# Threshold attention and a causal mixture of attention experts on one core: the mask moved from TensorE to VectorE, the threshold to GpSimd, the first pair in fp32, and a new order

## The chip, the cores and the metric

The kernel runs on one core of one Trainium2 chip. The metric is device time in microseconds (us), as a median of runs; lower is better. The engines are TensorE (PE in the rows; its weight loads are PEld), VectorE (DVE), ScalarE (ACT), GpSimd (POOL) and SyncE (SP), which issues the transfers (SPq is its queue).

## What is computed

Two attentions follow each other, for 8 batches. The first has 8 heads of 64 columns over 576 positions, and keeps only the scores within `tau` of the row's maximum. Its output, with the heads side by side, is the input of four expert attentions with a causal mask, of which each position takes the two that a gate ranks highest:

```python
scores = scale * q @ k.T
thresh = max(scores, -1) - tau
scores = where(scores >= thresh, scores, -1e9)
attn = exp(scores - max(scores)); attn /= sum(attn) + 1e-9
x = attn @ v                                  # heads side by side: 8 x 576 x 512
# experts e = 0..3, gate: two of four by x @ w_gate, softmax over the two
q, k, v = x @ wq[e], x @ wk[e], x @ wv[e]
scores = where(causal, -1e9, scale * q @ k.T)
a = exp(scores - max(scores)); a /= sum(a) + 1e-9
out += weight[e] * (a @ v @ wo[e])
```

All of it is fp32.

## The kernel before

The work of the first attention is cut into 32 pairs of heads (four pairs for each batch). A pair has nine head-tiles of 128 queries by 576 keys: four query tiles for each of two heads, and one tail tile that holds the last 64 queries of both. After four pairs comes the MoE stage of their batch: two pairs of experts, each with five query tiles.

`prep` loads and prepares a pair. To multiply in fp32r (a rounded fp32 that TensorE takes in one pass) without losing digits, each operand is transposed on TensorE and split into a high part (a ScalarE copy) and a low part (a VectorE subtraction), `hl`. Twelve SyncE transfers then spread them over the partitions, into `kt` (8) and `qt` (4). The query is scaled by `qsc` beforehand (`perm`, on GpSimd, for pair 0 on VectorE).

`scores` handles a head-tile: four matmuls (six for the tail tile, on `qd` and `hl`) into two banks of PSUM; a VectorE reduction gives the negated maximum (L525); a one-column VectorE operation gives the threshold `thr` (L517, `tau_p`); ScalarE takes the exp (L551); a VectorE operation with two inputs keeps exp where the score reaches the threshold and sums it (L539); after two heads VectorE inverts the sums (L515, L528) and GpSimd scales the tile (L517). `transp` transposes the result on TensorE and ScalarE copies it to `pt` (L488). `attnv` multiplies with the values.

`moe` runs `projected` and `values` (queries, keys, values, gate), `spread2` (transfers), then `scores2` for each tile: matmuls in fp32r; one bf16 matmul for each head adds the causal mask to the diagonal 128 columns, as `mask` times the identity `ident_b` (for the tail tile 64 columns of `mask2`); one reduction gives both heads' negated maxima; exp with a sum on ScalarE; inversion on VectorE; scaling by the gate on GpSimd. Then transposes, values, and `output`.

The order is not written by hand. Each operation goes into a list (`Plan.op`) with its engine and a guessed duration, from `cost`, `run`, `matmul` and `dma`. `Plan.arrange` then simulates five engines. TensorE takes its groups strictly by a rank, which is the pair's number plus an entry of `PLACE`; the others take the ready operation with the least rank (plus an entry of `PLACE_OP`). The program of each engine is what comes out, and on the chip each engine follows its own list in order. Buffers come from families with the counts in `SLOTS`; "s" is a tile of two banks, "g" of one.

Of the kernel before, what the change touches and what calls it, by code (L numbers as in the profile page):

```python
# [46 lines left out]
    "vload": 0.0126,  # L47
}
PLACE_OP = {
    "ACT gw": 0.9726, "ACT hl": 1.7382, "ACT lg": 0.8296, "ACT p2": -0.4951, "ACT pp": -0.1064, "ACT pt": -0.18,  # L50
    "ACT ptt": 0.0089, "ACT q2": -0.8434, "ACT q2d0": 0.5848, "ACT q2d1": 0.4564, "ACT v2": -0.3794,
    "ACT warm": -0.0714, "ACT wkh": -0.3286, "ACT woh": 0.3985, "ACT wqh": -0.7887, "ACT wvh": 0.8437,
    "ACT x": -0.737, "ACT z0": 0.6018, "ACT z1": 0.3857, "DVE col": 0.4443, "DVE gate": 0.6395, "DVE gt": -1.0307,
    "DVE gw": -0.8879, "DVE hl": -0.7751, "DVE lg": -0.0765, "DVE pp": -0.3478, "DVE pt2t": 0.6626,
    "DVE q2": 1.2382, "DVE qd0": -2.4916, "DVE qi": -1.5694, "DVE qsc": -0.8621, "DVE st": -0.6224,
    "DVE tau_p": 0.8442, "DVE tm": 1.5092, "DVE v2": 0.3515, "DVE warm": -0.6351, "DVE x": -1.4136,
    "DVE z0": 0.1452, "DVE z1": -0.7086, "POOL hl": -1.7102, "POOL ident": -0.1344, "POOL ident_b": 0.2099,
    "POOL ki": -0.3582, "POOL mask": -1.1453, "POOL mask2": -0.772, "POOL p2": 1.2822, "POOL pp": 0.981,
    "POOL q2d0": 0.2142, "POOL q2d1": 1.651, "POOL qd0": 0.9441, "POOL qd1": -0.1544, "POOL qi": 1.7205,
    "POOL st": 0.3311, "POOL tie": -0.8985, "POOL tm": 0.3736, "POOL vtz0": -0.1835, "POOL vtz1": -1.1581,  # L60
    "POOL wkl": 1.6919, "POOL wol": -0.3468, "POOL wql": 2.3927, "POOL wvh": -0.2524, "POOL wvl": 2.8955,
# [3 lines left out]
}  # L65
AV_GROUPS = ((4, 0, 1), (2, 3))
AV2_GROUPS = ((4, 3), (2, 1, 0))

# [319 lines left out]
def kernel(  # L388
# [670 lines left out]
    for n in range(NPR):  # L1059
        pair(n)  # L1060
        if n == 0:
            later()
            for c in range(NC):
                load_weights(c, 1.0 + 0.3 * c)
# [38 lines left out]
```

## Time and profile before

| | |
|---|---|
| median of 3 runs | 950.55 us (950.45 to 952.97) |
| the profiled execution | 949.99 us |
| its span, first to last instruction | 948.3 us |
| busy: TensorE / VectorE | 913.8 / 745.8 us |
| busy: ScalarE / GpSimd | 657.2 / 397.3 us |
| mean granted TensorE clock | 0.996 |

A busy share is an average over stages; what an edit is worth is read from the stage in which its instructions stand. Matmuls are pipelined: the duration of a row is from its start to its modelled end, and the spacing of starts tells what a slot costs. "Idle before" is the time in which the engine stood ahead of an instruction, with what ended it.

### The profile page before, as it was taken

How to read it: one execution, taken by the hardware profiler on the slowest of the kernel's cores; microseconds unless marked ns; L12 is line 12 of the kernel's file. 1: busy time of each engine (PE TensorE's matmuls, PEld its weight loads, DVE VectorE, ACT ScalarE, POOL GpSimd, SP SyncE). 2: the span in 40 equal slices, each digit the busy share in tenths (PEclk: the TensorE clock that was granted, in tenths of full speed). 3: DMA queues.
4: the chain of work that ended last, by engine and by line, in shares of the span. 5: the costliest groups of instructions: out<-in, count | busy, mean ns of one | idle time of the engine just before them, and what ended most of it. 6: DMA issues, size and time to landing. Idle time of an engine off the chain costs nothing.

```text
span 948.3 us, 26245 instructions
## 1 busy us (share of the span) xinstructions
PE 913.8 (96%) x9360; PEld 846.5 (89%) x9360; DVE 745.8 (79%) x2192; ACT 657.2 (69%) x1528; POOL 397.3 (42%) x664
## 2 busy tenths in 40 slices
PE   4798999999999999999999999999999999999998
PEld 3687999899999998999999999989999899999986
DVE  4799878887889868797878877888788886889254
ACT  3677777786678766787667866678566776678443
POOL 3674435453355434354244533445235443334122
PEclk9899999999999999999999999999999999999999
DMA  6766564545555453744636456354464645360151
GB/s 151 199 172 151 128 157 111 128 118 132 140 149 144 129 120 89 185 123 122 141 93 163 110 137 170 100 148 119 118 152 132 152 111 120 89 156 21 35 150 51
DMA packets 125122, 121.27 MB, mean 128 GB/s; under 512 B 67136, under 2 KB 83264, under 8 KB 124992
## 3 DMA queue, kind: packets, MB, share of 16 engines
q1 hardware_dynamic: 124992, 119.60, 50.3%
q8 instruction: 74, 1.21, 0.6%
q14 instruction: 56, 0.46, 0.1%
HBM read 30.42 MB, written 9.44 MB: 42 GB/s over the span
## 4 chain that ended last, share of the span: by engine, by line
PE 79%; DVE 10%; ACT 3%; SPq 3%; DMA 2%; issue 2%; POOL 1%; DVEq 0%; ACTq 0%; POOLq 0%
PE banks L468 60%; PE banks L1072 19%; DVE col L525 4%; DVE pp L539 3%; SPq L561 2%; ACT pt L488 1%; SPq L563 1%; ACT pp L551 1%; DMA st<-in_moe_wq_dram 1%; DMA k2x<-q 1%; DVE x L499 1%; DMA st<-in_moe_wk_dram 1%; DVE col L517 0%; DVE gt L490 0%; DVE col L515 0%
## 5 line engine op out<-in xcount | busy, mean ns | idle before, releaser
L517 POOL TENSOR_SCALAR pp<-pp,col 128x576 f32<-128x576 f32 x288 | 212.6, 749 | 271.2 <-DVE col L528 225.6
L525 DVE TENSOR_REDUCE col<-banks 128x1 f32<-128x576 f32 (+4 forms) x368 | 276.5, 761 | 56.2 <-PE banks L468 54.9
L551 ACT ACTIVATE pp<-banks,col 128x576 f32<-128x576 f32 (+2 forms) x296 | 215.2, 736 | 73.9 <-DVE col L525 60.4
L539 DVE SCALAR_TENSOR_TENSOR pp<-banks,col,pp 128x576 f32<-128x576 f32 x288 | 231.1, 814 | 38.1 <-ACT pp L551 32.9
L488 ACT ACTIVATE pt<-banks 128x512 f32<-128x512 f32 (+2 forms) x400 | 218.7, 588 | 48.7 <-PE banks L1072 46.7
L468 PE MATMUL banks<-kt,qt 128*128 128x288 f32 x1024 | 191.2, 317 | 7.6 <-DVE pp L539 3.8
L1072 PE MATMUL banks<-ident,pp 128*128 128x128 f32 x1326 | 192.0, 276 | 6.1 <-DVE pp L539 2.5
L1072 PEld LDWEIGHTS banks<-ident,pp 128*128 128x128 f32 x1326 | 154.9, 142 | 12.3 <-POOL pp L517 5.1
L468 PEld LDWEIGHTS banks<-kt,qt 128*128 128x128 f32 x1024 | 146.4, 193 | 19.1 <-DVE pp L539 5.5
L468 PE MATMUL banks<-pt,vm 128*64 128x128 f32 (+1 forms) x2560 | 155.1, 265 | 1.1 <-DMA vm<-in_v_dram 1.1
L468 PEld LDWEIGHTS banks<-pt,vm 128*64 128x64 f32 x2560 | 130.9, 137 | 9.7 <-issue 6.1
L517 POOL TENSOR_SCALAR p<-p,col,gw 128x512 f32<-128x512 f32 (+3 forms) x120 | 72.7, 614 | 97.6 <-DVE col L517 42.6
L551 ACT ACTIVATE p<-banks,col 128x512 f32<-128x512 f32 (+4 forms) x136 | 74.7, 555 | 30.3 <-DVE col L525 27.8
L468 PE MATMUL banks<-k2x,q2x 128*128 128x256 f32 (+3 forms) x256 | 62.2, 355 | 4.2 <-DMA k2x<-q 2.4
L468 PE MATMUL banks<-wvh,x 128*128 128x260 f32 x320 | 65.5, 288 | 0.0
L1072 PE MATMUL banks<-ident,p 128*128 128x128 f32 x386 | 60.4, 273 | 0.4 <-POOL p L517 0.3
L468 PE MATMUL banks<-woh,z 128*128 128x512 f32 x160 | 59.1, 413 | 1.5 <-DVE pp L539 1.5
L488 ACT ACTIVATE hl<-banks 128x512 fp32r<-128x512 f32 (+1 forms) x96 | 47.4, 494 | 18.2 <-PE banks L1072 13.3
L499 DVE TENSOR_TENSOR hl<-banks,hl 128x512 fp32r<-128x512 f32 (+1 forms) x96 | 52.8, 550 | 8.1 <-ACT hl L488 5.1
L468 PE MATMUL banks<-ptt,vtz 128*64 128x128 f32 (+1 forms) x640 | 59.0, 262 | 0.0
L517 DVE TENSOR_SCALAR col<-col,tau_p 128x1 f32<-128x1 f32 x288 | 55.4, 206 | 1.8
L468 PE MATMUL banks<-x,wkh 128*128 128x288 f32 x256 | 54.4, 304 | 0.0
(106 smaller groups left out, 1442.3 us busy)
## 6 DMA issues: line engine op xcount, KB each, us to landing
kt<-hl SPq DMA_DIRECT2D x256, 144.0 KB, 2.7
qt<-hl SPq DMA_DIRECT2D x128, 128.0 KB, 2.4
k2x<-q SPq DMA_DIRECT2D x128, 128.0 KB, 2.3
qi<-in_q_dram SPq DMA_DIRECT2D x64, 128.0 KB, 2.6
vm<-in_v_dram SPq DMA_DIRECT2D x32, 256.0 KB, 3.2
q2x<-q SPq DMA_DIRECT2D x64, 128.0 KB, 2.4
out_dram<-st SPq DMA_DIRECT2D x32, 256.0 KB, 2.4
km<-in_k_dram SPq DMA_DIRECT2D x31, 256.0 KB, 3.2
```

What stands on the lines that cost most here:

```text
L468: lambda o, x, y: nc.tensor.matmul(o, x, y, start=start, stop=stop))
L488: run(e, t, [dst], [src], lambda d, s: nc.scalar.activation(d, s, AF.Copy))
L499: lambda d, a, b: (nc.vector if e == "DVE" else nc.gpsimd).tensor_tensor(d, a, b, op=op))
L517: m.tensor_scalar(d, s, x_, y_, op0=op0, op1=op1)
L525: lambda d, s: nc.vector.tensor_reduce(d, s, axis=axis, op=op, **({"negate": True} if negate else {})))
L539: nc.vector.scalar_tensor_tensor(d, a_, x_, r.pop(0), op0=op0, op1=op1, **kw)
L551: nc.scalar.activation(d, s, AF.Exp, **kw)
L561: fn = lambda d, s: q_.dma_start(d.bitcast(F32), s.bitcast(F32))
L563: fn = lambda d: q_.dma_start(d, src)
L1072: o.fn(*(r.place() for r in (*o.outs, *o.ins)))
```

## The change

The causal mask is no longer a matmul. The query weights are negated, so that PSUM holds negated scores. For a tile of `scores2` one VectorE operation for each head adds the mask (now +1e9 above the diagonal, zeros before it, 512 columns wide), writes the sum back into PSUM and takes the minimum, which is the negated maximum that exp needs as its bias; exp then has the factor -1. The tail tile gets a VectorE addition of 64 columns, and a reduction as before. The threshold's one-column operation goes to GpSimd. Pair 0 is prepared by a new `first`: its operands are transposed and copied in fp32, without splitting and without spreading transfers, and each score half is one fp32 matmul; its query loads, and that of tau, are issued by ScalarE. The guessed durations change a little, `PLACE` may hold entries for a single pair (`s00@1`), and both tables of the order have new numbers.

```diff
@@ class Op
+        own = f"{self.unit}@{self.base:g}"
+        self.unit = own if own in PLACE else self.unit
@@ def matmul
-            t, more = 60, 145
+            t, more = 106, 145
+        elif w == HS and x.dtype == F32:
+            t, more = 4 * w * 0.43 + 9.5, 162
@@
+    def masked_min(s, m, least):
+        run("DVE", cost("DVE", size(s), True, True), [s, least], [s, m],
+            lambda o, a, i, m: nc.vector.tensor_tensor_reduce(o, i, m, 1.0, 3e38, ALU.add, ALU.min, a))
@@
-    mask = const("mask", [P, P], BF16)
+    mask = const("mask", [P, SM], BF16)
@@ def load_weights
-        for w, wh, wl, sc in ((wq, wqh, wql, SCALE), (wk, wkh, wkl, 1.0), (wv, wvh, wvl, 1.0)):
+        for w, wh, wl, sc in ((wq, wqh, wql, -SCALE), (wk, wkh, wkl, 1.0), (wv, wvh, wvl, 1.0)):
@@
+    def first():
+        plan.place = (-9.5, "load")
+        tl = plan.tile("tm", [P, 2, D], F32)
+        ki, qi = (plan.tile(f, [P, R, 2, D], F32) for f in ("ki", "qi"))
...
+        for j in range(2):
+            dma(ki[:, :, j], ks[:, :, j])
+            dma(qi[:, :, j], qs[:, :, j], "ACT")
+        dma(tl[ST:], k[0, :2, SM:, :].rearrange("h s d -> s h d"))
+        dma(tl[:ST], q[0, :2, SM:, :].rearrange("h s d -> s h d"), "ACT")
...
+        for x, name in ((ki, "kT"), (qi, "qT")):
...
+            for r in range(R):
+                transpose(g[:, r * P:(r + 1) * P], x[:, r].rearrange("p j d -> p (j d)"))
+            if x is ki:
+                copy("ACT", kx[:, ST:ST + SM], g)
+            else:
+                scaled("DVE", qx[:, :SM], g, qsc, 0.0, ALU.mult, ALU.add)
...
+        return (qx, kx, qd, None, *values_in(0))
@@ def scores
-            k_ = 2 if s < R else 3
+            k_ = 0 if n == 0 else 2 if s < R else 3
+            for hf in range(2 if n == 0 else 0):
+                sl = heads[j] if s < R else slice(0, P)
+                o = hf * HS + (ST if j == 0 else 0)
+                matmul(sp[:, hf, :HS], qt[sl, s * P:(s + 1) * P] if s < R else qd, kt[sl, o:o + HS], True, True)
@@
-            scaled("DVE", thr[:, js], nmx[:, js], -1.0, tau_p, ALU.mult, ALU.subtract)
+            scaled("POOL", thr[:, js], nmx[:, js], -1.0, tau_n, ALU.mult, ALU.add)
@@ def scores2
-                    matmul(g[:, j], q2x[:, j, t * P:w], k2x[:, j, i, :w], i == 0, False)
-                matmul(g[:, j, t * P:w], ident_b, mask, False, True)
+                    matmul(g[:, j], q2x[:, j, t * P:w], k2x[:, j, i, :w], i == 0, i == 1)
             views = [g[:, j] for j in range(2)]
-            reduce(nmx, g, AX.X, ALU.max, negate=True)
+            for j, sv in enumerate(views):
+                masked_min(sv, mask[:, SM - w:], nmx[:, j:j + 1])
...
-            matmul(g[:, 1, HS - ST:HS], ident_b, mask2, False, True)
+            edge = g[:, 1, HS - ST:HS]
+            tt("DVE", edge, edge, mask2, ALU.add)
...
-                reduce(nmx[:, :1], sv, AX.XY, ALU.max, negate=True)
+                reduce(nmx[:, :1], sv, AX.XY, ALU.min)
```

## Rows read from the trace of the kernel before

**Rows 1.** The page's first part: the span, then busy us of each engine.
```profile
span 948.3 us, 26245 instructions
PE 913.8 (96%) x9360; PEld 846.5 (89%) x9360; DVE 745.8 (79%) x2192; ACT 657.2 (69%) x1528; POOL 397.3 (42%) x664
```
**Rows 2.** Busy time by stage: window, length, engines, granted clock, DMA share, GB/s.
```profile
15.00:25.00 10.00, 7.54 (x29) 6.82 (x30) 7.01 (x19) 4.99 (x9) 3.80 (x8) 1.00 0.75 176
25.00:50.00 25.00, 19.93 (x185) 17.95 (x185) 19.44 (x57) 17.00 (x34) 17.98 (x28) 0.86 0.80 204
50.00:100.00 50.00, 45.15 (x495) 40.64 (x496) 46.01 (x140) 37.79 (x80) 29.73 (x53) 1.00 0.60 148
...
300.00:400.00 100.00, 99.54 (x1027) 93.78 (x1026) 80.19 (x241) 71.57 (x168) 41.62 (x67) 1.00 0.53 134
...
910.00:930.00 20.00, 18.09 (x158) 15.71 (x157) 11.50 (x31) 13.44 (x44) 7.84 (x12) 1.00 0.42 106
```
**Rows 3.** Timeline of TensorE: start, length, operation; the tail tiles of three pairs.
```profile
12.20 1.96 PE L468 MATMUL banks<-hl,qd 128*128 128x288 f32 x6 [0.78 <-POOL ki L517]
...
39.66 1.07 PE L468 MATMUL banks<-hl,qd 128*128 128x288 f32 x6
...
97.55 1.06 PE L468 MATMUL banks<-hl,qd 128*128 128x288 f32 x6
```
**Rows 4.** The clock: a one-microsecond stage, and matmuls early and late in the timeline.
```profile
29.00:30.00 1.00, 0.55 (x3) 0.55 (x4) 0.90 (x5) 0.44 (x1) 0.82 (x2) 0.50 0.92 247
...
21.16 3.32 PE L468 MATMUL banks<-kt,qt 128*128 128x288 f32 x12 [0.52 <-DVE hl L499]
...
29.45 4.32 PE L1072 MATMUL banks<-ident,pp 128*128 128x128 f32 x19 [2.46 <-DVE pp L539]
...
240.09 1.30 PE L468 MATMUL banks<-kt,qt 128*128 128x288 f32 x8
```
**Rows 5.** Groups by line and shape: count, busy us, mean ns, idle before and releasers.
```profile
L539 DVE SCALAR_TENSOR_TENSOR pp<-banks,col,pp 128x576 f32<-128x576 f32 x288 | 231.1, 814 | 38.1 <-ACT pp L551 32.9 <-issue 1.5
...
L517 POOL TENSOR_SCALAR pp<-pp,col 128x576 f32<-128x576 f32 x288 | 212.6, 749 | 271.2 <-DVE col L528 225.6 <-PE banks L1072 15.6 <-DVE col L515 15.1
...
L468 PE MATMUL banks<-mask,ident_b 128*128 128x128 bf16 x128 | 29.5, 230 | 0.0
...
L525 DVE TENSOR_REDUCE col<-banks 128x2 f32<-128x1024 f32 x16 | 19.5, 1220 | 3.0 <-PE banks L468 2.8
...
L517 POOL TENSOR_SCALAR wvh<-lg 128x4 fp32r<-128x4 f32 x4 | 0.8, 199 | 0.0
```
**Rows 6.** Timeline of TensorE around a mask matmul in the last MoE.
```profile
907.38 0.40 PE L468 MATMUL banks<-woh,z 128*128 128x512 f32 x1
907.61 0.40 PE L468 MATMUL banks<-wol,z 128*128 128x512 f32 x1
...
909.25 0.71 PE L468 MATMUL banks<-k2x,q2x 128*128 128x512 f32 x2
909.80 0.23 PE L468 MATMUL banks<-mask,ident_b 128*128 128x128 bf16 x1
909.84 0.48 PE L468 MATMUL banks<-k2x,q2x 128*128 128x256 f32 x2
```
**Rows 7.** Timeline of VectorE: a threshold and the reduction behind it.
```profile
24.55 0.21 DVE L517 TENSOR_SCALAR col<-col,tau_p 128x1 f32<-128x1 f32 x1
24.68 0.74 DVE L525 TENSOR_REDUCE col<-banks 128x1 f32<-128x576 f32 x1
```
**Rows 8.** Timeline: a GpSimd scale and a VectorE multiplication at the same time.
```profile
29.57 1.47 POOL L517 TENSOR_SCALAR pp<-pp,col 128x576 f32<-128x576 f32 x2 [0.18 <-DVE col L528]
29.69 0.82 DVE L539 SCALAR_TENSOR_TENSOR pp<-banks,col,pp 128x576 f32<-128x576 f32 x1
```
**Rows 9.** Timeline: the issue of the first query loads and their first use.
```profile
2.69 1.15 SPq L563 DMA_DIRECT2D qi<-in_q_dram  x2
...
6.06 0.49 DVE L517 TENSOR_SCALAR qi<-qi,qsc 128x512 f32<-128x512 f32 x1 [0.16 <-DMA qi<-in_q_dram]
```

More of the change, by code (lines that the diff above doesn't have):

```diff
@@ L55 @@
[L55 to L59, printed above, removed]
@@ L506, in scaled @@
         kx, ky = isinstance(x, Ref), isinstance(y, Ref)
-        t = cost(e, size(src), inps(src)) + (20 * kx + 80 * ky if e == "POOL" else 0)
+        t = cost(e, size(src), inps(src)) + (20 * kx + 80 * ky if e == "POOL" else 50 * ky)
         def fn(d, s, *r):
@@ L550, in fn @@
                 kw["bias"] = r.pop(0)
-            nc.scalar.activation(d, s, AF.Exp, **kw)
+            nc.scalar.activation(d, s, AF.Exp, scale=scale, **kw)
         run("ACT", cost("ACT", n, inps(src), accum is not None) + 80, [dst] + ([accum] if accum is not None else []),
@@ L558, in dma @@
         a, b = isinstance(dst, Ref), isinstance(src, Ref)
-        late = 2530 if a and b else 2950 if a else 2250
+        late = 2650 if a and b else 2950 if a else 2250
         if a and b:
@@ L581 @@
     run("POOL", 600, [ident], [], lambda x: make_identity(nc, x))
-    dma(tau_t, bass.AP(tensor=tau.tensor, offset=tau.offset, ap=[[0, P], [1, 1]]))
-    scaled("DVE", tau_p, tau_t, 0.0, op0=ALU.max)
+    plan.place = (-9.45, "load")
+    dma(tau_t, bass.AP(tensor=tau.tensor, offset=tau.offset, ap=[[0, P], [1, 1]]), "ACT")
+    plan.place = (-9.0, "load")
+    scaled("DVE", tau_n, tau_t, -1.0, 0.0, op0=ALU.mult, op1=ALU.min)
     scaled("DVE", qsc, tau_t, 0.0, SCALE, op0=ALU.is_ge, op1=ALU.mult)
@@ L608, in later @@
     def later():
-        plan.place = (0.2, "load")
-        rounded(ident_b, ident)
+        plan.place = (0.0, "later")
         memset("POOL", mask, 0.0)
-        run("POOL", 300, [mask], [mask], lambda o, i: nc.gpsimd.affine_select(
-            out=o, in_=i, compare_op=ALU.is_ge, fill=NEG, base=0, pattern=[[-1, P]], channel_multiplier=1))
+        run("POOL", 300, [mask[:, SM - P:]], [mask[:, SM - P:]], lambda o, i: nc.gpsimd.affine_select(
+            out=o, in_=i, compare_op=ALU.is_ge, fill=-NEG, base=0, pattern=[[-1, P]], channel_multiplier=1))
         memset("POOL", mask2, 0.0)
@@ L623, in later, with load_weights @@
             memset("POOL", t.bitcast(F32), 0.0)
[L625 to L626 removed]
+    def load_weights(c):
+        plan.place = (0.0, f"w{c}")
         sl = slice(c * P, (c + 1) * P)
[L628 removed]
+        for w, wh, wl, sc in ((wq, wqh, wql, -SCALE), (wk, wkh, wkl, 1.0), (wv, wvh, wvl, 1.0)):
             t = plan.tile("st", [P, E, D], F32)
@@ L644, in load_weights, with values_in @@
             minus("POOL", wol[:, c], t, woh[:, c].bitcast(F32))
+    def first():
+        plan.place = (-9.5, "load")
+        tl = plan.tile("tm", [P, 2, D], F32)
+        ki, qi = (plan.tile(f, [P, R, 2, D], F32) for f in ("ki", "qi"))
+        ks = k[0, :2, :SM, :].rearrange("h (p r) d -> p r h d", r=R)
+        qs = q[0, :2, :SM, :].rearrange("h (r p) d -> p r h d", r=R)
+        for j in range(2):
[3 more added lines that the diff above has]
+        dma(tl[:ST], q[0, :2, SM:, :].rearrange("h s d -> s h d"), "ACT")
+        plan.place = (0, "load")
+        kx = plan.tile("p2", [P, 2 * SM], F32)
+        qx = plan.tile("p2", [P, 2 * SM], F32)
+        qd = qx[:, SM:SM + P]
+        plan.place = (0, "perm")
+        memset("POOL", qd, 0.0)
+        for x, name in ((ki, "kT"), (qi, "qT")):
+            plan.place = (0, name)
+            g = gbank()
+            for r in range(R):
[4 more added lines that the diff above has]
+                scaled("DVE", qx[:, :SM], g, qsc, 0.0, ALU.mult, ALU.add)
+        plan.place = (0, "tT")
+        g = gbank()
+        transpose(g[:, :P], tl.rearrange("p j d -> p (j d)"))
+        for j, sl in enumerate(heads):
+            scaled("DVE", qd[sl, j * ST:(j + 1) * ST], g[sl, :ST], qsc[sl], 0.0, ALU.mult, ALU.add)
+        for o in (0, ST + SM):
+            copy("ACT", kx[:, o:o + ST], g[:, ST:P])
+        return (qx, kx, qd, None, *values_in(0))
+    def values_in(n):
+        b, hp = divmod(n, NPAIR)
+        plan.place = (n, "vload")
+        vm = plan.tile("vm", [P, 2, R, D], F32)
+        dma(vm, v[b, 2 * hp:2 * hp + 2, :SM, :].rearrange("h (p r) d -> p h r d", r=R))
+        for j, rows in enumerate((slice(0, ST), slice(ST, P))):
+            dma(vtz[n % 2][rows, j], v[b, 2 * hp + j, SM:, :])
+        return vm, vtz[n % 2]
     def prep(n):
         b, hp = divmod(n, NPAIR)
+        if n == 0:
+            return first()
         hs = slice(2 * hp, 2 * hp + 2)
@@ L654, in prep @@
             to = None
-            if sc is qsc or n == 0:
+            if sc is qsc:
                 to = plan.tile(name + "i", [P, R, 2, D], F32)
-                order_ = "h (r p) d -> p r h d" if sc is qsc else "h (p r) d -> p r h d"
-                src = x[b, hs, :SM, :].rearrange(order_, r=R)
+                src = x[b, hs, :SM, :].rearrange("h (r p) d -> p r h d", r=R)
                 for j in range(2):
                     dma(to[:, :, j], src[:, :, j])
-                if sc is qsc:
-                    plan.place = (n, "perm")
-                    fl = to.rearrange("p r j d -> p (r j d)")
-                    scaled("DVE" if n == 0 else "POOL", fl, fl, sc, 0.0, ALU.mult, ALU.add)
-                    plan.place = (n, "load")
+                plan.place = (n, "perm")
+                fl = to.rearrange("p r j d -> p (r j d)")
+                rounded(fl, fl, sc)
+                plan.place = (n, "load")
             else:
@@ L677, in prep @@
         plan.place = (n, "perm")
-        e = "DVE" if n == 0 else "POOL"
         ql = tl[:ST].rearrange("p j d -> p (j d)")
-        scaled(e, ql, ql, qsc[:ST], 0.0, ALU.mult, ALU.add)
+        scaled("POOL", ql, ql, qsc[:ST], 0.0, ALU.mult, ALU.add)
         hl = plan.tile("hl", [P, 2, 2 * SM + 3 * ST], F32R)
@@ L711, in prep @@
         split(slice(SM, SM + 2 * ST), g[:, :P])
-        e = "DVE" if n == 0 else "POOL"
-        copy(e, hl[:, :, KO + S:], hl[:, :, KO:KO + ST].bitcast(F32))
+        copy("POOL", hl[:, :, KO + S:], hl[:, :, KO:KO + ST].bitcast(F32))
         for j, sl in enumerate(heads):
-            copy(e, qd[sl, :, j * ST:(j + 1) * ST], hl[sl, :, SM:KO].bitcast(F32))
+            copy("POOL", qd[sl, :, j * ST:(j + 1) * ST], hl[sl, :, SM:KO].bitcast(F32))
         spread_keys(0)
@@ L721, in prep @@
         spread_queries(1)
-        plan.place = (n, "vload")
-        vm = plan.tile("vm", [P, 2, R, D], F32)
-        dma(vm, v[b, 2 * hp:2 * hp + 2, :SM, :].rearrange("h (p r) d -> p h r d", r=R))
-        for j, rows in enumerate((slice(0, ST), slice(ST, P))):
-            dma(vtz[n % 2][rows, j], v[b, 2 * hp + j, SM:, :])
-        return qt, kt, qd, hl[:, :, KO + ST:], vm, vtz[n % 2]
+        return (qt, kt, qd, hl[:, :, KO + ST:], *values_in(n))
     def inverse(x):
```

41 lines of the change are left out of this document (23 added, 18 removed), and 57 rows, old and new, of tables (PLACE, PLACE_OP).

## The prediction

> **What bounds the kernel now.** I read the page first: TensorE is busy for 913.8 of 948.3 us, VectorE for 745.8, ScalarE for 657.2, GpSimd for 397.3 [rows 1]. So the question is where TensorE is not fed, and the busy time by stage answers it. From 300 to 400 us, and so in all the middle, TensorE is busy 99.5% and VectorE about 80%: there every matmul slot taken away is time. From 25 to 100 us VectorE is busy about as long as TensorE (46.0 of 50 us from 50 to 100), with TensorE short of work [rows 2]. In the first 25 us nothing is full. From 910 to 930 us TensorE is at 90%, and chains through the other engines count.
>
> Then the landmarks. Each pair begins on TensorE with its tail tile (six matmuls banks<-hl,qd): the first at 12.20, the second at 39.66, the fifth at 97.55 us [rows 3]. So pair 0 takes 27.5 us, pairs 1 to 3 take (97.55 - 39.66) / 3 = 19.3 us each. Beside an MoE stage TensorE alone sets the pace; in these first 97 us something else does.
>
> Last, the clock. One stretch is shown at 0.50, half of full speed (1.2 in place of 2.4 GHz), after TensorE had stood still for some 2.5 us; the stage from 15 to 25 us is shown at 1.00. But twelve 288-column matmuls at 21.16 us took 3.32 us, 0.28 us each, where eight took 1.30 us, 0.16 us each, at 240 us [rows 4]. By durations the clock was low for most of the head, whatever the column says. I go by durations. The Trainium skill (TensorE: Matmul & The Clock Gate, Part 1) has the low clock as the state before activity; the durations agree, the granted column does not; by the column the sum below would be some 3 us lower.
>
> **The change part by part.** *Mask matmuls (128 of 128 columns, 16 of 64) go from TensorE.* The 230 ns of one in the groups [rows 5] is latency, not cost. Cost is the spacing: two 512-column matmuls start 0.23 us apart, so the pair that starts at 909.25 has given its slots by 909.71; the mask starts at 909.80 and the next matmul at 909.84 [rows 6]. That is 0.09 + 0.04 = 0.13 us with the switch to bf16 and back; I take 0.125. Ends: 0.04 (the start-to-start alone, 5.8 us in all) and 0.23 (the whole latency, 33 us). 126 of them lie in the seven batches beside another pair: 126 x 0.125 = 15.8 us. 18 lie in the last MoE, where TensorE partly waits [rows 2]; I count half, 1.1 us. Together 16.9 us.
>
> *What VectorE takes on.* 64 tiles had one reduction over two heads (1.22 us at 2 x 512 columns); now two masked minima write the scores back. The operation is not in the trace. Below it lies the reduction for the same columns (no change), above it two of the 814 ns passes with two inputs and a sum (2 x 576 columns, 1.63 us) [rows 5]. It has two inputs, so I take the upper side, +0.3 us: 64 x 0.3 = 19 us. 16 additions of 64 columns: some 0.2 us each, 3 us. Both stand beside TensorE work in seven batches, where VectorE has about 20% to spare [rows 2]: nothing on the path. In the last MoE the first head's minimum ends earlier than the joint reduction did, the second's later: nothing either way. Cover gone, it would cost 22 us.
>
> *The threshold (288 one-column operations) goes from VectorE to GpSimd.* On VectorE it lasts 0.21 us but the next reduction starts 0.13 us after it [rows 7], so 288 x 0.13 = 37 us are freed. VectorE's net is -15, about 731 us. On GpSimd the nearest row is four columns in 199 ns [rows 5]: 288 x 0.2 = 58 us, and GpSimd comes to 455 us, half of the span. It adds a wait: the masked multiplication (L539) now waits for ScalarE's exp and for GpSimd. Exp takes about as long as one 749 ns GpSimd scale, so a threshold that finds GpSimd inside a scale ends up to 0.2 us late; behind the waiting multiplication on VectorE stand the next tile's reduction, and behind that TensorE, which wants the bank. In the middle the spare of VectorE hides it. In pairs 1 to 3, where VectorE is the pace, nine thresholds less per pair are 9 x 0.13 = 1.2 us, three pairs 3.6 us. Ends: 0 (it comes back as waits) and 3 x (19.3 - 16) = 10, TensorE's own pace for a pair being about 16 us (38 matmuls of 288 columns at 0.133, 50 transposes at 0.11, the values' some 5.5; an estimate from the spacing at full clock).
>
> A row speaks on sharing: a multiplication that ran at 29.69 us beside a GpSimd scale lasted 0.82 us [rows 8], the mean over all being 814 ns with GpSimd busy 42%. The Trainium skill (Perfetto Trace Analysis, Optimizing Scalar/DVE Operations) warns that VectorE and GpSimd share an SBUF port, so that moving work between them may not help. By it the 3.6 us would be nothing and the sum 3.6 us higher; these rows show no such loss for these operations.
>
> *First pair in fp32.* Before, each operand is split in two on ScalarE and VectorE, copied by twelve SyncE transfers, and the keys are loaded after the queries: the query loads were issued at 2.69 to 3.84 and used at 6.06 us [rows 9], the first scores start at 12.20, and pair 0 gives way at 39.66. After, SyncE issues three key loads, ScalarE three query loads beside them; a load used 2.2 us after its issue has ended should be there at about 5 us. (ScalarE issues no load in the trace; taken as SyncE's, the ends below hold the rest.) Transposes, about 1 us at the low clock, and one evacuation, 0.7, for each operand: scores from about 7.8 us, an estimate. A tile is now two fp32 matmuls in place of four; each lies between one and four times the 0.133 us of before, and the diff itself charges four, so I take 1.0 us a tile, 2.0 at the low clock. Three tiles at 2.0 until the clock is up, then VectorE's pace, some 1.5 us (0.75 + 0.81 + 0.09, overlapping): 7.8 + 6.0 + 6 x 1.5 = 22.8, and 2.3 for the last tile's reduction, exp and multiplication: 25. Then pair 1's own splitting on VectorE (1.7) and TensorE's backlog of transposes: pair 1's tail tile at about 29 in place of 39.66, so 10.7 us. Ends: 2 (low clock throughout, backlog at half speed) and 14 (full clock from the start). That SyncE is free of pair 0's twelve transfers costs nothing and lets pair 1's loads go first.
>
> *Signs, mask width, weights' place.* Negated query weights and exp with a factor -1 are the same instructions. The wider mask is written once by GpSimd, under 1 us, long before use: nothing. The new weight positions load on SyncE and GpSimd in the same head; hidden as before.
>
> *The new order.* It cannot be priced from the trace. Where TensorE is 99.5% busy it can hardly win; it could lose or win some 4 us over seven batches (about 0.5 each). I take nothing.
>
> Sum on the profiled execution (949.99 us, 1.7 us more than its span, 0.06% under the median of 950.55): 949.99 - 16.9 - 10.7 - 3.6 = 918.8; I say 919.
>
> **The rivals.** (1) *The head is not shortened*: fp32 scores at the low clock hold TensorE, pair 1 still waits for its transfers, and only 2 us come. 949.99 - 16.9 - 2 = 931. For it: the low clock in the head. Against: VectorE was idle for 5.6 of the 25 us from 25 to 50 [rows 2], so an earlier start is worth something. 14%. (2) *The threshold brings no relief*, VectorE waiting for GpSimd what it saves: 922.4. For it: GpSimd's scales are as long as the exp. 10%. (3) *The head comes to TensorE's pace*: 14 + about 8 us in place of 10.7 + 3.6, so 911 or less. For it: with VectorE lighter, TensorE has the most work of all. 15%. (4) *Slower*: the threshold stands in GpSimd's strict order behind a scale that itself waits, so each of the 288 multiplications starts d late. VectorE then has 731 + 288 d; with the about 25 us at both ends in which it cannot work, it passes 950 from d = 0.67 us. A whole scale, 0.75, gives 731 + 216 + 25 = 972. For it: a GpSimd scale of 749 ns is longer than d, and nothing overtakes it. Against: GpSimd is idle for half the span, and the order can put the threshold ahead of a scale that waits. 5%, of which 1% ends near no change.
>
> **How the numbers follow.** Forecast 56%: 919, its own range 912 to 926. For 8 in 10, I take in rivals 1 to 3 and the unknown order: 907 to 932; the mask's ends (5.8 to 33 us) lie partly beyond. A measurement of this kernel can tell about 0.3%. Faster: 95%. Within 0.3%: 1%. Slower: 4%.
>
> **What would show it.** Mask: the batch period on TensorE falls by 18 x 0.125 = 2.3 us. Head: pair 1's tail tile near 29, the fifth near 83 us, pairs 1 to 3 at about 18.1 us. Threshold: VectorE near 731 us, GpSimd near 455, and no GpSimd among the releasers of L539's multiplication; if it is there with many us, rival 2 or 4 holds. Masked minimum: two of 512 columns under 1.7 us together. The prediction is wrong if the middle's TensorE idle grows beyond 1%, or if the low clock comes back after the head.

## The result, and the profile after

The changed kernel takes 943.88 us (median of 5 runs, 942.60 to 947.33); the kernel before took 952.84 us beside it (950.45 to 954.02). The ratio is 0.9911, 95% interval 0.9892 to 0.9930: 0.9% faster. The prediction said 919, with 907 to 932 as its range: right in sign, and wrong by 25 us.

The profiled execution took 944.42 us. The page's first part, which answers [rows 1]:

```profile
span 942.7 us, 26180 instructions
PE 906.0 (96%) x9214; PEld 840.6 (89%) x9214; DVE 731.0 (78%) x2107; ACT 651.9 (69%) x1528; POOL 471.2 (50%) x952
```

TensorE lost 7.8 us of busy time and the span 5.6 us. VectorE fell to 731.0 us, as forecast; GpSimd rose to 471 (forecast 455). So the work moved as planned, but the time did not follow. That VectorE's sum came out to the microsecond is partly luck: the thresholds are worth 29.2 us of its time (e3 below, 760.2 with them), not 37, and the mask's move 17.5 (e1, 763.3 against 745.8), not 22. Busy time by stage (window, length, PE, PEld, DVE, ACT, POOL, granted clock, DMA share, GB/s), against [rows 2]:

```profile
25.00:50.00 25.00, 20.21 (x189) 16.55 (x190) 18.32 (x47) 16.16 (x34) 19.10 (x38) 0.91 0.69 166
50.00:100.00 50.00, 44.97 (x460) 40.75 (x461) 38.56 (x98) 34.98 (x71) 29.86 (x64) 0.90 0.53 128
...
200.00:300.00 100.00, 98.31 (x1008) 92.39 (x1007) 80.24 (x232) 70.22 (x167) 48.47 (x97) 1.00 0.51 126
300.00:400.00 100.00, 99.83 (x1026) 94.32 (x1025) 81.62 (x240) 72.20 (x172) 50.01 (x102) 1.00 0.54 134
```

The middle is about as full as before. From 25 to 100 us TensorE has no more busy time than before (65.2 us against 65.1), at a lower granted clock in the longer stretch: 0.90 from 50 to 100 us, where it was 1.00. The landmarks of [rows 3] show the same (TensorE's timeline: start, length, operation). The first line is pair 0's first scores, the next two the tail tiles of pairs 1 and 4, the last two those of the first pair of the third and of the eighth batch (pairs 8 and 28):

```profile
9.13 1.32 PE L484 MATMUL banks<-p,p 64*128 64x288 f32 x2 [1.07 <-ACT p L504]
...
31.79 0.40 PE L484 MATMUL banks<-hl,qd 128*128 128x288 f32 x1
...
101.78 0.29 PE L484 MATMUL banks<-hl,qd 128*128 128x288 f32 x1
...
206.91 0.29 PE L484 MATMUL banks<-hl,qd 128*128 128x288 f32 x1
...
765.92 0.29 PE L484 MATMUL banks<-hl,qd 128*128 128x288 f32 x1
```

The last two stand at these times in the kernel before:

```profile
203.44 0.40 PE L468 MATMUL banks<-hl,qd 128*128 128x288 f32 x1
...
768.65 0.40 PE L468 MATMUL banks<-hl,qd 128*128 128x288 f32 x1
```

Pair 1 begins 7.9 us earlier than before, and pair 4 begins 4.2 us later. The five batch periods in between last (765.92 - 206.91) / 5 = 111.80 us in place of 113.04, so a batch is 1.24 us shorter, where 2.3 was forecast. From the last of these lines to the end of the span it is 176.8 us in place of 179.6. The head is most of the 25 us: it gave 4 us away where 14 were to be won. The batches gave half of their forecast in this profile.

In the head TensorE stands still three times for a tile that is not yet scaled (timeline of TensorE; in brackets the idle time before and its releaser). L1134 are the transposes, L533 the scaling on GpSimd; for the first of them the matmul's row names VectorE's L531, which ended at the same time, and the row of its weight load names the scaling:

```profile
24.98 1.54 PE L1134 MATMUL banks<-ident,pp 128*128 128x128 f32 x6 [3.60 <-DVE col L531]
27.18 2.07 PE L484 MATMUL banks<-p,p 64*128 64x288 f32 x8
49.81 4.77 PE L1134 MATMUL banks<-ident,pp 128*128 128x128 f32 x19 [2.75 <-POOL pp L533]
70.32 1.12 PE L1134 MATMUL banks<-ident,pp 128*128 128x128 f32 x4 [3.05 <-POOL pp L533]
```

After each, the granted clock is at the lower level (1.2 GHz): the windows read 0.50.

```profile
25.00:28.00 3.00, 2.76 (x11) 2.00 (x13) 0.15 (x1) 1.26 (x4) 1.51 (x3) 0.50 0.69 153
50.00:54.00 4.00, 3.97 (x18) 3.27 (x18) 0.63 (x4) 2.15 (x6) 2.32 (x4) 0.50 0.76 182
70.00:73.00 3.00, 2.68 (x12) 2.69 (x13) 1.72 (x6) 0.90 (x2) 2.63 (x5) 0.50 0.93 224
```

What GpSimd did before the first of these waits, and who waited for it:

```profile
21.25 0.74 POOL L515 TENSOR_TENSOR wvl<-st,wvh 128x256 fp32r<-128x256 f32 x1 [0.90 <-ACT wvh L504]
21.96 1.26 POOL L515 TENSOR_TENSOR wol<-st,woh 128x512 fp32r<-128x512 f32 x1
23.21 0.27 POOL L533 TENSOR_SCALAR col<-col,tau_n 128x1 f32<-128x1 f32 x1
23.55 0.82 DVE L555 SCALAR_TENSOR_TENSOR pp<-banks,col,pp 128x576 f32<-128x576 f32 x1 [0.81 <-POOL col L533]
```

Two weight splits hold GpSimd for 2 us; the threshold stands behind them, and the masking multiplication behind the threshold. Before the second and the third wait GpSimd does other work: the second scaling follows 0.21 us of idleness, the third follows copies for a coming pair (`hl`, `qd`) and a threshold:

```profile
49.01 1.47 POOL L533 TENSOR_SCALAR pp<-pp,col 128x576 f32<-128x576 f32 x2 [0.21 <-DVE col L544]
...
68.50 0.67 POOL L508 TENSOR_SCALAR qd<-hl 64x128 fp32r<-64x128 f32 x2
```

So there were three suspects: the threshold in GpSimd's queue, the weight splits, and the order that puts these transposes where it does. For the batches there were two: that a mask matmul costs TensorE less than I took, and that the masked minimum on VectorE makes TensorE wait.

### The profile page after: what moved, and what is told of

It is laid out like the page before. It is cut to its first block, busy times and chain, and to the rows that moved or that the text cites. A ratio compares the mean times of both kernels' runs of the same rounds, so it can differ in the third digit from the quotient of the medians.

```text
span 942.7 us, 26180 instructions
## 1 busy us (share of the span) xinstructions
PE 906.0 (96%) x9214; PEld 840.6 (89%) x9214; DVE 731.0 (78%) x2107; ACT 651.9 (69%) x1528; POOL 471.2 (50%) x952
## 4 chain that ended last, share of the span: by engine, by line
PE 77%; DVE 8%; DMA 4%; ACT 4%; issue 3%; POOL 3%; SPq 1%; ACTq 0%; DVEq 0%; POOLq 0%
PE banks L484 57%; PE banks L1134 20%; DVE pp L555 2%; DMA kt<-hl 2%; DVE col L541 2%; DMA qi<-in_q_dram 2%; ACT pp L571 1%; SPq L581 1%; POOL pp L533 1%; ACT pt L504 1%; ACT p L571 1%; DVE col L531 0%; DVE x L515 0%; DVE hl L515 0%; POOL col L533 0%
## 5 line engine op out<-in xcount | busy, mean ns | idle before, releaser
L533 POOL TENSOR_SCALAR pp<-pp,col 128x576 f32<-128x576 f32 x288 | 212.6, 748 | 164.3 <-DVE col L544 113.9
L541 DVE TENSOR_REDUCE col<-banks 128x1 f32<-128x576 f32 x304 | 225.7, 753 | 49.4 <-PE banks L484 45.7
L571 ACT ACTIVATE pp<-banks,col 128x576 f32<-128x576 f32 (+1 forms) x295 | 215.0, 744 | 61.2 <-DVE col L541 52.3
L1134 PE MATMUL banks<-ident,pp 128*128 128x128 f32 x1331 | 197.1, 280 | 16.3 <-POOL pp L533 10.0
L484 PE MATMUL banks<-kt,qt 128*128 128x288 f32 x992 | 184.8, 313 | 5.4 <-DMA kt<-hl 4.5
L1134 PEld LDWEIGHTS banks<-ident,pp 128*128 128x128 f32 x1331 | 154.9, 143 | 33.7 <-POOL pp L533 18.4
L533 POOL TENSOR_SCALAR col<-col,tau_n 128x1 f32<-128x1 f32 x288 | 76.8, 267 | 160.3 <-DVE col L541 149.8
L571 ACT ACTIVATE p<-banks,col 128x576 f32<-128x576 f32 (+4 forms) x137 | 74.7, 551 | 14.6 <-DVE col L531 6.4
L533 POOL TENSOR_SCALAR p<-p,col,gw 128x384 f32<-128x384 f32 (+3 forms) x122 | 73.7, 612 | 18.3 <-ACT pp L571 5.7
L504 ACT ACTIVATE x<-banks 128x256 fp32r<-128x256 f32 (+1 forms) x96 | 28.3, 329 | 70.6 <-PE banks L484 70.6
L515 DVE TENSOR_TENSOR q<-banks,q 128x288 fp32r<-128x288 f32 x64 | 29.0, 452 | 44.7 <-ACT q L504 44.2
L560 DVE CUSTOM_DVE_ANT_0 banks<-banks,mask 128x512 f32<-128x512 f32 (+3 forms) x128 | 61.9, 499 | 1.6
L1134 PE MATMUL banks<-ident,p 128*128 128x128 f32 x381 | 61.1, 276 | 0.9 <-POOL p L533 0.9
```

The costliest lines, as they stand in the source:

```text
L484: lambda o, x, y: nc.tensor.matmul(o, x, y, start=start, stop=stop))
L504: run(e, t, [dst], [src], lambda d, s: nc.scalar.activation(d, s, AF.Copy))
L515: lambda d, a, b: (nc.vector if e == "DVE" else nc.gpsimd).tensor_tensor(d, a, b, op=op))
L533: m.tensor_scalar(d, s, x_, y_, op0=op0, op1=op1)
L541: lambda d, s: nc.vector.tensor_reduce(d, s, axis=axis, op=op, **({"negate": True} if negate else {})))
L560: lambda o, a, i, m: nc.vector.tensor_tensor_reduce(o, i, m, 1.0, 3e38, ALU.add, ALU.min, a))
```

## The experiments

All of them compare with the kernel before on the same chip. The code of the edits is shortened. Unless told otherwise, the order of all instructions on every engine is that of the kernel it is made from, so that one thing changes. Times are medians; a difference between two experiments is taken from their ratios to the kernel before, times 950 us; behind ± stands what the two intervals together leave open.

| kernel | us | before beside it | ratio, 95% interval |
|---|---|---|---|
| changed kernel | 943.88 | 952.84 | 0.9911 (0.9892 to 0.9930) |
| e1_mask_alone | 948.80 | 951.36 | 0.9977 (0.9962 to 0.9991) |
| e2_mask_and_threshold | 969.77 | 951.36 | 1.0192 (1.0171 to 1.0212) |
| e3_threshold_back | 943.67 | 951.36 | 0.9914 (0.9895 to 0.9934) |
| e4_filled_waits | 939.27 | 951.36 | 0.9867 (0.9853 to 0.9881) |
| e5_no_mask | 943.68 | 950.48 | 0.9926 (0.9900 to 0.9953) |
| e6_mask_twice | 955.66 | 950.48 | 1.0061 (1.0036 to 1.0085) |
| e7_splits_twice | 950.28 | 950.48 | 1.0001 (0.9990 to 1.0012) |
| e8_head_reordered | 940.24 | 952.07 | 0.9877 (0.9858 to 0.9897) |
| e9_reordered_and_filled | 940.64 | 952.07 | 0.9886 (0.9866 to 0.9906) |
| e10_split_old_places | 954.72 | 949.97 | 1.0051 (1.0035 to 1.0067) |
| e11_fp32_old_places | 948.63 | 949.97 | 0.9981 (0.9968 to 0.9995) |

**e1: the mask alone, in the old order.**

```diff
-                matmul(g[:, j, t * P:w], ident_b, mask, False, True)
+                # not issued
-            reduce(nmx, g, AX.X, ALU.max, negate=True)
+            # per head: tensor_tensor_reduce(sv, sv, mask, 1.0, 3e38, ALU.add, ALU.min, nmx)
```

> The kernel before, in its own order on every engine; only the causal mask is moved: the mask matmuls of the mixture layers are not issued, the weights of the second queries are negated, and VectorE does two masked minimums where it did one maximum (an addition and a minimum in the tail tile). Theory 1 (the mask's price in the sum was right, the loss is in the head): 16.9 us less than before, some 934 (932 to 937). Theory 2 (the masked minimum lengthens the chain from the second scores to their transposes, so the TensorE time saved is waited away): 942 to 949, and TensorE's waits for the GpSimd scaling of the second probabilities grow. Theory 3 (the new order is what lost the gain): as theory 1, and this kernel is faster than the changed one by 5 us or more.

948.8 us, 2.2 us less than before: theory 1 fell here, and theory 3 with it. The time is that of theory 2, but its wait is not there: TensorE waits 0.7 us for the scaling of the second probabilities, where it was 0.3. TensorE's busy time fell to 906.2 us as in the changed kernel, but the span did not. Where a step was lost, in the MoE stage of the second batch:

```profile
288.09 0.59 PE L468 MATMUL banks<-k2x,q2x 128*128 128x384 f32 x2
289.52 0.41 PE L468 MATMUL banks<-k2x,q2x 128*128 128x384 f32 x1 [0.84 <-ACT pt L488]
290.25 0.41 PE L468 MATMUL banks<-k2x,q2x 128*128 128x384 f32 x1 [0.31 <-DMA k2x<-q]
```

The matmuls that followed at once before now wait for a bank and for a transfer. The order was made for the old timing: TensorE arrives earlier and waits there. Its time without work grew from 34.5 us (948.3 - 913.8) to 43.1 (949.3 - 906.2).

**e5 and e6: the mask's price on TensorE.** In e5 the masks are not issued and nothing replaces them; in e6 each is issued twice.

```diff
             if x.dtype == BF16:
+                nc.tensor.matmul(o, x, y, start=start, stop=False)
```

> The kernel before in its own order, without the mask matmuls and with nothing in their place: the second layer's scores stay unmasked, so the causal mask is left out of what is computed. This gives the price of the 144 mask matmuls on TensorE by itself. By the prediction (0.125 us each in 126 cases): 16.9 us less than before, some 934 to 936. By the steps of 0.06 to 0.07 us per mask that the kernel with the mask alone shows against the kernel before: 8 to 10 us less, 941 to 944. What lies between this time and that of the kernel with the mask alone (948.8) is what the masked minimum costs in that order: 5 to 8 us.

> The kernel before in its own order, with each of the 144 mask matmuls issued twice (masked scores are lower by the constant twice, nothing else differs). By the prediction's price of 0.125 us: 17 to 18 us above before, some 969. By 0.06 to 0.07 us each: 8 to 10 us above, some 960.

Without masks the kernel is 7.0 us faster (4.5 to 9.5), with twice as many 5.8 us slower (3.4 to 8.1). Both medians lie below the lower of the two expectations (8 to 10). In the time of the whole kernel 144 masks are worth 6 to 7 us, 0.04 to 0.05 us each, and not 16.9.

On TensorE itself a mask takes more than that. In the last MoE eight matmuls run without idle time between `woh,z` and `x,wkh`, first with four masks among them (the kernel before, further lines in [rows 6]), then with none (e5):

```profile
908.75 0.61 PE L468 MATMUL banks<-k2x,q2x 128*128 128x512 f32 x2
...
910.56 0.51 PE L468 MATMUL banks<-x,wkh 128*128 128x288 f32 x2
```

```profile
904.88 1.54 PE L468 MATMUL banks<-k2x,q2x 128*128 128x512 f32 x8
906.26 0.43 PE L468 MATMUL banks<-x,wkh 128*128 128x288 f32 x2
```

1.81 us against 1.38: 0.43 for four masks, 0.11 each. Part of it comes behind the mask: two matmuls directly behind one take longer than two that follow a matmul of their own kind (0.71 us at 909.25 against 0.61 at 908.75, 0.51 against 0.43 for `x,wkh`). The two programs issue the same matmuls in the same order but for the masks; over the 135 masks with no idle time beside them in either trace, the starts give 0.09 us each, some 13 us for 144. A second mask takes less, as no such switch is added (e6):

```profile
278.86 0.23 PE L469 MATMUL banks<-mask,ident_b 128*128 128x128 bf16 x1
278.93 0.22 PE L470 MATMUL banks<-mask,ident_b 128*128 128x128 bf16 x1
```

It starts 0.07 us behind the first here, 0.06 in other places. The Trainium skill (TensorE: Matmul & The Clock Gate, "Wait — 56ns, not 53.3ns?") gives some 56 ns from start to start for 128 columns at the full clock; these starts lie a little above it. So e6 prices a mask beside a mask, and e5 the mask.

Why e5 gains 7 us and not 13: TensorE has 11.3 us less busy time than before, and its time without work grew by 6.6 us, from 34.5 to 41.1 (943.6 - 902.5); its waits for the keys' transfer into `k2x` alone grew from 2.4 to 5.3 us:

```profile
PE 902.5 (96%) x9216; PEld 840.7 (89%) x9216; DVE 746.2 (79%) x2192; ACT 656.6 (70%) x1528; POOL 397.3 (42%) x664
```

The masked minimum in the old order costs e1 less e5, 0.51% or 4.8 us (± 2.9; expected 5 to 8). So in e1 what the mask's removal brings and what its replacement costs nearly cancel.

**e2 and e3: the threshold.** e2 adds the threshold on GpSimd to e1, at the place where VectorE had it; e3 does the reverse in the changed kernel.

```diff
-            scaled("POOL", thr[:, js], nmx[:, js], -1.0, tau_n, ALU.mult, ALU.add)
+            nc.vector.tensor_scalar(thr, nmx, -1.0, tau_n, op0=ALU.mult, op1=ALU.add)   # e3, same place
```

> As the kernel with the mask alone, still in the order of the kernel before, and the threshold goes from VectorE to GpSimd at the same place of the order. Theory 1: 0 to 4 us less than with the mask alone (the term of 3.6 us for pairs 1 to 3, or nothing where TensorE is the bound). Rival (the threshold in GpSimd's queue is what cost the gain): 3 us or more above the mask alone, with TensorE waiting for the scaled tile behind it.

> The changed kernel in its own order, but the threshold is computed on VectorE again. Theory 1 (GpSimd's weight splits and the order make the three waits of the head): the waits at 21, 47 and 67 us stay; VectorE has 288 small instructions more; 944 to 948. Rival (the threshold in GpSimd's queue costs the gain): 930 to 941, the new wait of the masking multiplication for GpSimd (13.6 us in all) gone and with it most of the three waits of TensorE.

e2 is 20 us slower than e1, far beyond what I expected of the rival. Its waits of VectorE, and its middle (engine, tile and line of the waiting group, releaser: us in all, times, longest):

```profile
DVE pp L539 <- POOL col L772: 31.8, 48, 2.7
300.00:400.00 100.00, 97.66 (x983) 91.00 (x980) 77.70 (x230) 69.61 (x165) 49.04 (x99) 1.00 0.48 119
```

In an order not made for the move, GpSimd meets the threshold late: that is the cause that rival 4 of the prediction named. That its figure (972) lies close to the 969.77 us measured here is luck. It had VectorE full and each of the 288 multiplications starting 0.75 us late; here 48 of them wait, 31.8 us in all or 0.11 us a multiplication, and VectorE is busy 77.7 of 100 us in the middle. In the changed kernel, whose order was made for it, the same group waits 13.6 us:

```profile
DVE pp L555 <- POOL col L533: 13.6, 13, 1.7
```

And there the move is worth nothing. With the threshold back on VectorE (760.2 us busy) the time is 943.67 us against 943.88 (by the ratios 0.3 us more, ± 2.6; theory 1 had said 944 to 948), and the three waits stay as they were (TensorE's waits from 12 to 110 us):

```profile
PE banks L1135 <- POOL pp L533: 9.8, 8, 3.1
PE banks L1135 <- DVE col L531: 4.0, 1, 4.0
```

So the threshold is not what spoils the head in this order; the first suspect is out.

**e7: the weight splits.** Each low half of the weights is computed twice on GpSimd.

```diff
-            minus("POOL", wl[:, c, :E * D], tf, wh[:, c, :E * D].bitcast(F32))
+            twice(wl[:, c, :E * D], tf, wh[:, c, :E * D].bitcast(F32))   # same tensor_tensor, issued two times
```

> The changed kernel in its own order, but GpSimd makes each low half of the weights in the head twice over (16 subtractions of 0.74 to 1.26 us more, 13 to 14 us of GpSimd time). If GpSimd's weight work in front of the scaling is what makes TensorE's three waits of the head: these waits grow together by 3 us or more and the time by 3 to 8 us, 947 to 952. If the waits come from the place that the order gives to the three transposes, and GpSimd has room: within 1 us of the changed kernel, 943 to 945.

950.28 us, 0.9% or 8.6 us (± 2.1) above the changed kernel. GpSimd has 14 subtractions and 10.9 us more (482.1 us against 471.2), less than the 16 and 13 to 14 expected. TensorE's waits for a scaled tile from 12 to 110 us grow from 12.7 to 20.0 us, first the changed kernel (with the first wait under L531's name), then e7:

```profile
PE banks L1134 <- POOL pp L533: 9.1, 7, 3.0
PE banks L1134 <- DVE col L531: 3.6, 1, 3.6
```

```profile
PE banks L1140 <- POOL pp L533: 20.0, 9, 4.7
```

So GpSimd has no room in the head: 10.9 us more of its work cost 8.6. That the splits as they stand make the three waits does not follow, and the rows above speak against it. For the first wait the inverted sums were there at 22.74 us and the scaling began at 23.46, so a split and the threshold held it for 0.7 of the 3.60 us; no split stands right ahead of the other two scalings.

**e4: the clock after the waits.** Transposes of the identity are put ahead of the three transposes that wait.

```diff
+    fill = {118: 30, 424: 24, 673: 26}    # first transposes of pair 0, 1 and 2 that wait
...
             o = plan.ops[n]
+            for _ in range(fill.get(n, 0)):
+                x = ident.place()
+                nc.tensor.transpose(o.outs[0].place(), x, x)
```

> The changed kernel, but ahead of the three transposes of the head for which TensorE stood idle (21.4, 47 and 67 us) it transposes the identity 30, 24 and 26 times into the same bank, which the real transposes then overwrite; all else as in the changed kernel. If the low clock after each wait is a loss of its own: the stretch after each runs at full rate, 4 to 8 us less, 936 to 940. If the engines ahead of TensorE set the pace of the head anyhow, so that the low clock costs nothing: 943 to 945, and the time goes into longer waits.

939.27 us, 0.44% or 4.2 us (± 2.2) less than the changed kernel, though TensorE does 80 transposes more. The stretches of 0.50 are at 1.00 (the last line is the timeline behind the first of them); in the head a lower reading is left ahead of them, 0.66 from 20 to 25 us:

```profile
25.00:28.00 3.00, 2.61 (x23) 2.21 (x22) 0.59 (x2) 0.98 (x2) 2.09 (x4) 1.00 0.65 146
50.00:54.00 4.00, 2.94 (x25) 2.61 (x24) 0.68 (x1) 2.75 (x8) 2.25 (x4) 1.00 0.61 138
70.00:73.00 3.00, 2.55 (x22) 2.31 (x21) 2.38 (x5) 2.58 (x6) 2.70 (x7) 1.00 0.87 211
27.50 1.25 PE L484 MATMUL banks<-p,p 64*128 64x288 f32 x8
```

The same eight fp32 matmuls take 1.25 us here, and 2.07 us above. So each of these waits cost itself and then the low clock behind it, which is a loss of its own. The planner in this file charges a wait as a wait, with the same matmul costs after it.

**e8 and e9: another order of the head.** e8 changes only the constants in `PLACE` for pairs 0 to 3, for the loads and for the weights; e9 adds one filling of 24 transposes.

```diff
+PLACE.update({"s20@0": ..., "t01@1": ..., "load@2": ..., "w0": ..., ...})   # pairs 0 to 3 and weights only
```

> The changed kernel with the same instructions; only the places in the order of the first four pairs, of the weights and of the loads in the head are others. They were chosen so that, with TensorE at half rate after each long wait counted in, the planner leaves one wait of TensorE above 2 us in the head (before the transposes of pair 0's second tile) in place of three. If the order of the head is what lost the gain: the fifth tail tile at 90 to 94 us in place of 101.78, the low clock after 47 and 67 us gone, 932 to 937. If the head is bound by the work of the engines and the order only moves the waits: 941 to 945.

> As the reordered head, and 24 transposes of the identity ahead of the one transposition for which TensorE still waits over 2 us. If the low clock after a long wait is a loss of its own: 1 to 2.5 us less than with the reordered head alone. If what follows that wait is bound by other engines: the same time within 0.5 us.

e8 takes 940.24 us, 3.2 us (± 2.6) less than the changed kernel, between the two expectations. Its profile has one wait above 2 us behind the start in place of three (3.87 us); its fifth tail tile starts at 98.99 us in place of 101.78, not at 90 to 94. So the order holds part of the loss, and the expectation was too high. e9 gained nothing over e8 (ratios 0.9886 and 0.9877): in its profile the fifth tail tile comes at 97.60 us, 1.4 us earlier, and the gain goes between pairs 6 and 7, where TensorE waits for the spread keys and then runs some 3.4 us at the lower clock, as it does not in e8's profile (1.00 from 170 to 185 us):

```profile
175.68 0.50 PE L515 MATMUL banks<-kt,qt 128*128 128x288 f32 x2 [1.59 <-DMA kt<-hl]
177.00:181.00 4.00, 4.00 (x56) 4.00 (x56) 3.21 (x9) 0.74 (x1) 1.18 (x3) 0.57 0.37 115
```

**e10 and e11: the first pair, and what the new order is worth.** Both have the changed kernel's mask and threshold, and the planner works with the places of the kernel before; e10 prepares the first pair as before, e11 in fp32.

```diff
+PLACE.update({...}); PLACE_OP.update({...})    # e10, e11: the values of the kernel before
-        if n == 0:                             # e10 only: prep() of the kernel before
-            return first()
```

> The changed kernel with the first pair prepared as before (operands split in two, four matmuls a tile) and with the table of places of the kernel before, from which the planner makes an order that keeps pair after pair in sequence. The mask and the threshold are as in the changed kernel. It is the partner of the next run, which has the first pair in fp32 and the same table. In the head: fifth tail tile near 97 us, as in the kernel before (97.55). Time 945 to 955, since this table was not made for these instructions.

> The same table of places, with the first pair straight in fp32. If the fp32 first pair is worth what the prediction said, once the head keeps its sequence: pair 0 ends and every later pair begins 8 to 11 us earlier than in the partner, and the time is as much lower. If the head is not shortened whatever the order (rival 1): 0 to 3 us. What the changed kernel's new table gave away in the head is then the difference of its fifth tail tile (101.78) to this run's: 10 us or more by the first, less than 5 by the second.

The tail tiles of pairs 1 and 4, first e10, then e11; the last two lines of e11 are the third and eighth batch (pairs 8 and 28):

```profile
42.04 1.14 PE L486 MATMUL banks<-hl,qd 128*128 128x288 f32 x6
102.31 1.06 PE L486 MATMUL banks<-hl,qd 128*128 128x288 f32 x6
```

```profile
34.81 1.07 PE L486 MATMUL banks<-hl,qd 128*128 128x288 f32 x6
95.76 1.06 PE L486 MATMUL banks<-hl,qd 128*128 128x288 f32 x6
201.85 0.40 PE L486 MATMUL banks<-hl,qd 128*128 128x288 f32 x1
765.83 1.06 PE L486 MATMUL banks<-hl,qd 128*128 128x288 f32 x6
```

e10 missed one of its expectations: its fifth tail tile stands at 102.31 us, not near 97. With the first pair in fp32, pair 1 begins 7.2 us earlier and pair 4 6.6, and 0.70%, 6.7 us (± 2.0), of it reaches the end: between the two expectations (8 to 11, and 0 to 3). In this order the head keeps its sequence, and pair 4 begins 6.0 us earlier than in the changed kernel. But the batches are longer: (765.83 - 201.85) / 5 = 112.80 us against 111.80. So the changed kernel's new places lose 6.0 us in the head and buy 1.0 us in each batch until, at pair 28, both stand level (765.83 and 765.92). What they gain comes behind it, in the last batch and its MoE stage: e11 takes 181.1 us from there to the end of its span (946.9), the changed kernel 176.8. By the ratios they gain 0.70%, 6.7 us (± 2.2); these two profiles show 4.2.

That makes a chain from before to after, by ratios times 950 us: mask and threshold moved, with the old places, +4.8; first pair in fp32, -6.7; new places, -6.7; sum -8.5. The forecast for these three steps was -20.5, -10.7 and 0. The first step holds also that the old places did not fit the new instructions; its whole loss is there when pair 4 begins (102.31 against 97.55 us).

## Why the prediction was wrong

What the sum left out is the order: which saved time reaches the end, and which new wait arises, depended on places that I priced at nothing. Term by term:

*The mask matmuls (16.9 us) failed at the step from TensorE's slot to the kernel's time, and in part by size.* I wrote that in the middle every matmul slot taken away is time, as TensorE is 99.5% busy there. The slot itself was read nearly right: 0.11 us in the last MoE and 0.09 in the mean, where I took 0.125, some 13 us in all (only the 0.09 us that I placed ahead of a mask belong to the mask before, behind which matmuls start late). But with the masks out and nothing in their place 7.0 us reach the end (e5); 6.6 us came back as waits. The end I called lower, 5.8 us, lies near that by luck: its 0.04 us leaves out the late start behind the mask.

*The masked minimum (0 on the path) failed in the old order, and its price in the new one is not shown.* Its own duration was inside the bound: 698 ns for 512 columns, two 1.40 us, and 1.68 with the read of the accumulator behind each, under the 1.7 forecast.

```profile
L560 DVE CUSTOM_DVE_ANT_0 banks<-banks,mask 128x512 f32<-128x512 f32 x32 | 21.8, 698 | 0.2
L560 DVE DVE_READ_ACCUMULATOR2_ANT col<- 128x1 f32 x128 | 18.0, 141 | 0.0
```

I argued that VectorE's spare of 20% hides it. e1 shows that spare is no cover where the order is fixed: 4.8 us came back as waits. In the changed kernel a batch is 1.24 us shorter, 0.07 us for each of its 18 masks; with the old places and the same instructions (e11) it is 0.24 us shorter. Five other kernels with the changed kernel's places in the batches (e3, e4, e7, e8, e9) have periods of 110.9 to 111.3 us, 1.8 to 2.1 us shorter than before, so the forecast of 2.3 was nearer than this one profile says. With an order made for it most of the mask's price is had, and without one hardly any; how much of it is the mask and how much the places no run tells apart.

*The first pair (10.7 us) had the right mechanism and the wrong size.* First scores at 9.13 us (forecast 7.8), pair 1 at 31.79 (29): each step a little short. Worth 6.7 us (e10, e11). I also called the clock low for most of the head; by the same durations it is low to about 25 us and from 29 to 35, and full behind that (six matmuls in 1.96 us at 12.20, in 1.07 at 39.66 [rows 3]).

*The landmark itself misled.* I took the start of a pair's tail tile for the end of the pair before. In the changed kernel the order starts pair 1 while much of pair 0 is left: pair 0's first multiplication with the values stands at 37.88 us, 6 us behind pair 1's tail tile, where it stood ahead of it before (36.75 and 39.66). 101.78 us for pair 4 is what counts, and the forecast for it was 83.

*Thresholds in pairs 1 to 3 (3.6 us) failed: the term is 0 (e3, 0.3 us ± 2.6).* VectorE was not the pace of these pairs in the new order: with the thresholds back it is busy 39.73 of 50 us from 50 to 100 us, without them 38.56, and the time is the same. That is rival 2 in effect. Of the two explanations that I had, waits for GpSimd and the shared port, the rows bear out the first only for another order (e2). For the port: in the kernel before, the masking multiplications that run wholly beside GpSimd work last 815 ns in the mean, those with none beside them 814. So the warning of the Trainium skill (Perfetto Trace Analysis, "Optimizing Scalar/DVE Operations") does not show in their duration here; its conclusion, that such a move may not help, holds.

GpSimd's one-column operation with a column operand took 267 ns in the mean, against 200 taken from the four-column row [rows 5], hence 471 us in place of 455; nothing hung on it.

*The new order (0) is the term that I had to price and did not.* I kept 4 us for it either way over seven batches, and none for the head. With the same instructions the new places lose 6.0 us before pair 4 begins (e11), gain them back in the batches, and gain some 4 us more at the end. In the head they put TensorE in front of tiles that are not yet scaled; filling the three waits gave 4.2 us back (e4), other places for the head 3.2 (e8). I wrote that the new weight positions are hidden as before: e7 shows that GpSimd has no room for more of that work there, and how much the splits cost as they stand is not shown. The rows spoke of it: [rows 4] shows a wait of 2.46 us in the kernel before, and 19 transposes at half rate behind it. I used that for the clock of the head and did not ask which new waits the change could make there.

*Signs that I had named.* The low clock did come back, within the head. GpSimd does stand among the releasers of the masking multiplication, with 13.6 us. The middle's idle grew past 1% in some stages (1.7% from 200 to 300 us, where it was 0.2%), by waits for the spread keys' transfer, such as

```profile
291.13 0.50 PE L484 MATMUL banks<-kt,qt 128*128 128x288 f32 x2 [1.58 <-DMA kt<-hl]
```

What stays open: why mask and threshold with the old places lose 4.8 us in the head (e10), and why pairs 1 to 3 take no less than before with thresholds off VectorE, (95.76 - 34.81) / 3 = 20.3 us each in e11, 20.1 in e10 and 19.3 before. No engine is full there, and no one wait is left that explains it.

The fastest kernel here is e4, 939.27 us (0.9867), the changed one with the three waits filled; e8 comes to the same within the intervals (0.9877).

## What to carry to other kernels

Price a removed matmul by what its neighbours' spacing becomes without it, those behind it too, over many places; then ask what the other engines do when TensorE comes that much earlier, for here only half of it reached the end. When a kernel's order is planned, a moved operation has no price of its own: the same threshold cost 20 us in the old order and nothing in the new one, so cost the order, first of all where the engines are not full. A TensorE wait of some 3 us was paid twice here, once as the wait and once at half rate behind it; filling three such waits with idle matmuls gave 4.2 us, and filling one in another order (e9) gave nothing in the end.

## What the runs showed of the hardware that I had not expected

- Waits of 2.75 to 3.60 us on TensorE were each followed by the granted clock of 0.50; with transposes of the identity in their place it stayed at 1.00 from 25 to 28, 50 to 54 and 70 to 73 us, and the kernel gained 4.2 us. A wait of 1.59 us was followed by the lower clock in e9 (0.57 from 177 to 181 us), one of 1.58 us in the changed kernel was not (1.00 from 200 to 300 us).
- A bf16 mask of 128 columns between fp32r matmuls takes 0.09 us of TensorE's time in the mean, part of it as a later start of the matmuls behind it; a second mask directly behind the first adds 0.06 to 0.07. One is shown with 230 ns.
- The fp32 score matmuls of one head (64 rows, four in the trace) take as long as those of two heads (eight), which use the two halves of the rows: 1.23 us in the changed kernel, 1.25 us in e4 above.

```profile
20.16 1.23 PE L484 MATMUL banks<-p,p 64*128 64x288 f32 x4
```

- VectorE and GpSimd side by side: the masking multiplication takes 814 ns in the mean with GpSimd busy for 50% of the span, 813 ns in e3 with 42%.
